# Inverse row sums of attention: turned by VectorE in 32x32 blocks and spread through DRAM, instead of turned by TensorE

## The chip, the cores and the metric

The program runs on one core of one Trainium2 chip. The metric is the device time of one execution in microseconds (us), median of several runs. Engines are named as in the profile: PE (TensorE, matmuls), PEld (its weight loads), DVE (VectorE), ACT (ScalarE), POOL (GpSimd), SP (SyncE, whose queue issues most transfers).

## The reference

Clustered attention, then two feed-forward layers. Batch 2, 8 heads, 768 tokens, head size 64, 16 clusters per head:

```
q_n, k_n, c_n = q, k, centroids, each row divided by (its norm + 1e-6)
mask    = argmax(q_n . c_n) == argmax(k_n . c_n)          # query and key in the same cluster
scores  = where(mask, q . k / 8, -1e9)
attn    = exp(scores - max(scores))
attn    = attn / (sum(attn) + 1e-9)                        # the row sums of this text
x       = (attn @ v) as [1536, 512]
x       = relu(x @ w_in)**2 @ w_out                        # first layer, 512 -> 2048 -> 512
out     = gelu_sigmoid(x @ w2_in) @ w2_out                 # second layer
```

## The kernel before

Sixteen (batch, head) problems are worked as 8 pairs of heads; a pair has two halves of 384 queries each, so there are 16 halves, n = 0 to 15. A half has three tiles of 128 queries for each of its two heads: six groups, 96 in all. Even n is the first half of a pair, odd n the second.

For each group PE multiplies queries by keys (`scores`, L615, and with the rest of the operands and the cluster masks as further rows L618), DVE takes the row maximum (`peak`, L624), ACT the exponential with the row sum beside it (`exponents`, L632), PE turns the 128x128 blocks of the exponentials (`turn`, L640), DVE and ACT copy them out of PSUM (`keep`, L648), and PE multiplies them by v (`values`, L658), into one PSUM bank for the half, with 64 partitions for each head and 384 columns for the queries.

The division by the row sum comes last. The sums of a half lie with queries on partitions: six columns, one for each group. The product lies with queries on columns. So the inverse sums must be turned and then copied to the 64 partitions of their head. Before, this is done in five steps: DVE adds 1e-9 and takes the reciprocal (`inverse`, L663 and L664); POOL copies each column 64 times side by side, 128x384 (`spread`, L669); PE turns that in three 128x128 transposes into a PSUM bank (`ratio`, L675); ACT copies the bank to a tile `rb` of 128x384 (`ratio_out`, L679); DVE multiplies the product by it on its way out of PSUM (`whole`, L696). `rb` has two buffers, and in some halves it also holds the result, which POOL's subtractions (`t_sum_first`, L715) read later.

Beside this runs the preparation of later pairs (`prep`): loads of q, k and v (L355), casts on ACT whose result is copied to other partitions by SP's transfers (`k_high` L443/L444, `q_high` L453/L454), subtractions on POOL (`k_low` L448, `q_low` L458), assignments to clusters (`aff` L476 and L479 on PE, `aff_out` L485 on ACT, `back` L493 on PE, `back_out` L503), a square root as a power on POOL (`root`, L507), the inverse norms (`inv_norm`, L513 and L514), `scale` (L526, POOL), `most` (L534), `less` (L537, POOL), `first`, `least`, `one_hot` (L541, L545, L552), `mask` (L559) and `mask_out` (L575 on ACT, then four copies by SP, L580).

The order on each engine is written by hand: every step has a key, in units of a group (about 2.3 us), and all steps are issued in the order of the keys; each engine takes its own in that order, and SP its transfers. Keys of a half are relative to `ORIGIN + 6 * n`, those of a pair to `12 * p`. Waits between engines are put in by the framework, by the memory that steps read and write. PSUM has two double-bank tiles for scores ("S") and four single banks ("T") for all else in this stage, the transposes of `ratio` among it.

After the attention both layers are matmuls from end to end, with the weights rebuilt from 64-bit words on ACT, DVE and POOL. The weights of the first layer begin to come in (L266) while the last pairs are still at work.

Of the kernel before, what the change touches and what calls it, by code (L numbers as in the profile page):

```python
# [8 lines left out]
F32 = mybir.dt.float32  # L9
# [7 lines left out]
P = 128  # L17
# [9 lines left out]
    scores=(0.0, 0.3), peak=(0.5, 0.7), exp=(0.85, 1.5), turn=(2.64, 2.85, 3.06), keep=(3.3, 3.2, (3.6, 3.8)),  # L27
)
HALVES = dict(
    values=(9.3, 9.6, 11.3, 11.6, 13.3, 13.6), inverse=(7.4, 6.02), spread=(7.45, 6.03), ratio=9.85, ratio_out=10.15,  # L30
    whole=13.95, whole_high=14.0, whole_low=15.0,
)
PAIR = dict(
# [1 line left out]
    aff=(-15.15, -15.1), aff_out=(-14.95, -14.8), back=(-13.15, -13.1), back_out=(-12.95, -12.8),  # L35
    k_high=(-13.4, -6.9), k_low=(-12.95, -6.3), q_high=(-12.6, -10.7), q_low=(-12.2, -8.9),
    root=-12.7, inv_norm=-9.95, scale=-9.9, most=-8.98, less=-8.95, first=-6.98,
    least=-6.95, one_hot=-6.0, mask=(-5.15, -5.1), mask_out=(-4.95, -4.8),
)

LAST = dict(
    values=(97.1, 97.2, 97.3, 97.4, 97.5, 97.6), inverse=(95.9, 95.9), spread=(96.2, 96.2), ratio=97.05, ratio_out=97.4,
    whole=97.95, whole_high=98.0, whole_low=98.62,
)
FIRST = dict(
# [5 lines left out]
    one_hot=-48.0, mask=(-47.9, -47.7), mask_out=(-47.859, -47.659, -47.559, -47.459), table=-48.107,  # L51
# [31 lines left out]
def cluster_attention_then_two_ffns(  # L83
# [17 lines left out]
    nc = tc.nc  # L101
    B, H, D, S = q_t.shape
    C = centroids.shape[0] // H
    DM = H * D
    NT = S // P
    HALF = S // 2
    TH = NT // 2
    NP = H // 2
    PAIRS = [(b, hp) for b in range(B) for hp in range(NP)]
    NH = B * H  # L110
# [196 lines left out]

    with tc.manual_schedule():
        with ExitStack() as actx, ExitStack() as rctx:
            psum = actx.enter_context(tc.tile_pool(name="psum", bufs=1, space=bass.MemoryType.PSUM))  # L310
            def ps_s(name):
                return psum.tile([P, 2, 512], F32, tag="S", name=name, bufs=2)
# [4 lines left out]
            one = places  # L317
            two = Twice(places)
# [42 lines left out]
            load(0, "k")  # L361
            half = one.tile([P, NT, 2, 2], F32, name="half")
            nc.vector.memset(half, 0.5)
            unit = one.tile([P, 1], F32, name="unit")
            nc.scalar.activation(out=unit, in_=half[:, 0, 0, 0:1], func=AF.Sqrt)

# [60 lines left out]
            def at(key, f, *args):  # L427
                events.append((key, len(events), lambda: f(*args)))
# [172 lines left out]
            s_t, m_t, p_t, sum_t, pt_t, tp_t = {}, {}, {}, {}, {}, {}  # L601
# [47 lines left out]
                    out=pt_t[n][:, 4 * b:4 * b + 4, i * P:(i + 1) * P],  # L649
                    in_=tp_t.pop((k, b)).rearrange("p (a f) -> p a f", a=4))  # L650

            pv_t, rb_t = {}, {}

            def values(n, t):
                if t == 0:
# [3 lines left out]
                                     rhs=pt_t[n, j][:, t, :], start=(t == 0), stop=(t == NT - 1), skip_group_check=True)  # L659

            def inverse(n):
                rc = rb_t[n] = two.tile([P, NT], F32, tag="rc", name="rc", bufs=2)
                nc.vector.tensor_scalar_add(rc, sum_t[n], 1e-9)  # L663
                nc.vector.reciprocal(rc, rc)  # L664

            def spread(n):
                rc = rb_t[n]
                wide = rb_t[n] = two.tile([P, NT, D], F32, tag="wide", name="wide", bufs=1)
                nc.gpsimd.tensor_copy(out=wide, in_=rc.unsqueeze(2).to_broadcast([P, NT, D]))  # L669
# [62 lines left out]
            for k in range(NG // 2):  # L732
                begin = ORIGIN + 2 * k
# [3 lines left out]
                for b in range(3):  # L737
                    at(begin + GROUP["turn"][b], turn, k, b)
                    when = GROUP["keep"][b]
                    at(begin + (when if b < 2 else when[k % 2 == 0]), keep, k, b)  # L740
            for n in range(NH):
                when, begin = (LAST, 0.0) if n == NH - 1 else (HALVES, ORIGIN + 6 * n)
                for t in range(NT):
                    at(begin + when["values"][t], values, n, t)
                for name, f in (("inverse", inverse), ("spread", spread), ("ratio", ratio), ("ratio_out", ratio_out),
                                ("whole", whole), ("whole_high", whole_high), ("whole_low", whole_low)):
                    if n % 2 == 0 or n % 8 > 3 or name[:6] != "whole_":
                        late_low = name == "whole_low" and n % 8 in (5, 7) and n < NH - 1
                        at(begin + (when[name][n % 2] if name in ("inverse", "spread") else when["whole"] + 0.7 if late_low else when[name]), f, n)
                if n % 2:  # L750
                    for i, name in enumerate(("T1",) if n % 8 < 4 else ("T2", "T3", "T4")):
                        at(begin + when["whole"] + (T_SUM_LAST[i] if n == NH - 1 else T_SUM + 0.1 * i), t_sum_first, n, name)
# [307 lines left out]
            for j in range(MJ):  # L1060
# [8 lines left out]
                else:  # L1069
                    t = u0 + 14 * BLOCK * (j - 1)  # L1070
# [8 lines left out]
            _, done = second_hidden(u1)  # L1079

            jobs = []
            for m in range(MF):
                jobs.append((y0 - 5 + 2 * m, 0, 1, m))
                j, i = divmod(m, 2)
# [7 lines left out]
            for j in range(MJ):  # L1092
                add, split12, split34 = sums_of(j)
                if j == 0:
                    begin = (y0 + 39, y0 + 46.1, y0 + 47.1)
                elif j == 1:
                    begin = (u1 + 2.3, u1 + 0.5 * (done["P5", 0] + 0.3), u1 + 0.5 * (done["P3", 0] + 0.3))
                else:
                    s = u1 + 0.5 * done["P4", j - 2]
                    begin = (s + 4.6, s + 5.2, s + 5.6)  # L1100
# [14 lines left out]
            for layer, begin in enumerate((y0, y1)):  # L1115
                u, n = begin, 0
# [72 lines left out]
```

## Time and profile before

| | us |
|---|---|
| median of 3 runs | 758.69 |
| lowest and highest | 757.93, 758.74 |
| profiled execution | 758.31 |
| its span | 756.5 |
| PE busy in the span | 746.7 (99%) |
| DVE busy | 526.5 (70%) |
| ACT busy | 461.2 (61%) |
| POOL busy | 166.3 (22%) |

Times of engines come from the profiled execution; the span runs from its first to its last instruction, and what lies around it makes the rest of its 758.31 us. A busy PE is not PE at its peak: matmuls are pipelined, so the time from one matmul's start to the next counts, not the duration of one. The clock granted to PE is full in all 40 slices of the span.

### The profile page before, as it was taken

How to read it: one execution, taken by the hardware profiler on the slowest of the kernel's cores; microseconds unless marked ns; L12 is line 12 of the kernel's file. 1: busy time of each engine (PE TensorE's matmuls, PEld its weight loads, DVE VectorE, ACT ScalarE, POOL GpSimd, SP SyncE). 2: the span in 40 equal slices, each digit the busy share in tenths (PEclk: the TensorE clock that was granted, in tenths of full speed). 3: DMA queues.
4: the chain of work that ended last, by engine and by line, in shares of the span. 5: the costliest groups of instructions: out<-in, count | busy, mean ns of one | idle time of the engine just before them, and what ended most of it. 6: DMA issues, size and time to landing. Idle time of an engine off the chain costs nothing.

```text
span 756.5 us, 10808 instructions
## 1 busy us (share of the span) xinstructions
PE 746.7 (99%) x4010; PEld 607.5 (80%) x4010; DVE 526.5 (70%) x939; ACT 461.2 (61%) x799; POOL 166.3 (22%) x139
## 2 busy tenths in 40 slices
PE   8899999999999999999999999999999999999998
PEld 6677776767767799999988888888888888888886
DVE  6886866867897667765787769754777677776321
ACT  7877777786787478776844435554656565443321
POOL 4765756775749130000000000000000000000000
PEclk9999999999999999999999999999999999999999
DMA  5132321322330122200232320100212212230201
GB/s 190 43 105 59 94 80 43 96 64 72 94 92 2 59 108 63 106 20 37 84 106 89 112 84 19 39 28 29 84 56 84 83 56 93 102 113 29 111 1 55
DMA packets 16900, 54.53 MB, mean 72 GB/s; under 512 B 2576, under 2 KB 2576, under 8 KB 15824
## 3 DMA queue, kind: packets, MB, share of 16 engines
q1 hardware_dynamic: 16560, 53.19, 22.1%
q8 instruction: 31, 0.51, 0.3%
q10 hardware_dynamic: 288, 0.66, 0.2%
q14 instruction: 21, 0.17, 0.1%
HBM read 43.02 MB, written 3.15 MB: 61 GB/s over the span
## 4 chain that ended last, share of the span: by engine, by line
PE 92%; DVE 4%; ACT 2%; POOL 1%; issue 0%; DVEq 0%; POOLq 0%; ACTq 0%
PE bank L996 35%; PE row L807 13%; PE bank L884 10%; PE ps_v L658 8%; PE ps_p L640 7%; PE bank L893 6%; PE ps_s L615 5%; PE ps_s L618 4%; DVE arena L624 2%; PE ps_aff L476 1%; PE ps_h L807 1%; ACT arena L632 1%; PE ps_r L675 1%; PE warm L392 1%; PE ps_back L493 1%; PE ps_oh L559 1%
## 5 line engine op out<-in xcount | busy, mean ns | idle before, releaser
L996 PE MATMUL bank<-arena 128*128 128x512 f32 x1152 | 261.6, 389 | 0.0
L996 PEld LDWEIGHTS bank<-arena 128*128 128x128 f32 x1152 | 216.2, 188 | 45.0 <-DVE arena L983 0.2
L624 DVE TENSOR_SCALAR_CACHE_REDUCE arena<-ps_s 128x768 bf16<-128x768 f32 x96 | 91.7, 955 | 38.6 <-PE ps_s L618 11.1
L979 ACT CAST arena<-arena 128x512 fp32r<-128x512 f32 x96 | 59.5, 620 | 86.0 <-PE bank L996 85.6
L807 PE MATMUL row<-arena 128*128 128x384 f32 x630 | 109.7, 334 | 0.4 <-ACT arena L825 0.4
L807 PEld LDWEIGHTS row<-arena 128*128 128x128 f32 x630 | 109.2, 188 | 0.7 <-ACT arena L825 0.7
L632 ACT ACTIVATE arena<-ps_s,arena 128x768 f32<-128x768 f32 x96 | 87.1, 908 | 35.1 <-DVE arena L624 34.8
L983 DVE TENSOR_TENSOR arena<-arena,arena 128x512 fp32r<-128x512 f32 x96 | 66.1, 689 | 60.3 <-ACT arena L979 60.0
L884 PE MATMUL bank<-arena 128*128 128x512 f32 x336 | 80.9, 389 | 0.0
L884 PEld LDWEIGHTS bank<-arena 128*128 128x128 f32 x336 | 63.1, 188 | 13.1
L658 PE MATMUL ps_v<-arena 128*64 128x384 f32 x384 | 72.3, 498 | 0.0
L640 PE MATMUL ps_p<-arena 128*128 128x128 f32 x576 | 70.8, 272 | 0.0
L244 ACT CAST arena<-arena 128x512 fp32r<-128x512 f32 x48 | 29.8, 620 | 64.4 <-DVE arena L240 64.4
L640 PEld LDWEIGHTS ps_p<-arena 128*128 128x128 f32 x576 | 65.7, 141 | 2.3 <-issue 0.6
L615 PE MATMUL ps_s<-arena 128*128 128x384 f32 x192 | 54.9, 367 | 2.4 <-ACT arena L632 2.2
L247 DVE TENSOR_TENSOR arena<-arena,arena 128x512 fp32r<-128x512 f32 x48 | 33.2, 692 | 24.0 <-ACT arena L244 23.2
L618 PE MATMUL ps_s<-arena 80*128 80x384 f32 x192 | 49.8, 340 | 0.1
L893 PE MATMUL bank<-arena 128*128 128x512 f32 x192 | 48.1, 389 | 0.0
L615 PEld LDWEIGHTS ps_s<-arena 128*128 128x128 f32 x192 | 31.0, 189 | 20.3 <-ACT arena L632 10.6
L648 DVE COPY arena<-ps_p 128x512 f32<-128x512 f32 x72 | 47.0, 678 | 0.2 <-PE ps_p L640 0.2
L658 PEld LDWEIGHTS ps_v<-arena 128*64 128x64 f32 x384 | 23.4, 136 | 25.5 <-issue 25.4
L648 ACT COPY arena<-ps_p 128x512 f32<-128x512 f32 x72 | 41.9, 582 | 0.5 <-PE ps_p L640 0.5
(135 smaller groups left out, 950.6 us busy)
## 6 DMA issues: line engine op xcount, KB each, us to landing
arena<-in_w_dram SPq DMA_DIRECT2D x48, 512.0 KB, 3.2
arena<-in_w_dram SPq DMA_DIRECT2D x8, 1024.0 KB, 4.9
arena<-arena SPq DMA_DIRECT2D x32, 192.0 KB, 2.5
arena<-in_k_t_dram SPq DMA_DIRECT2D x8, 384.0 KB, 4.0
arena<-in_v_dram SPq DMA_DIRECT2D x8, 384.0 KB, 3.2
out_dram<-arena SPq DMA_DIRECT2D x11, 256.0 KB, 2.1
arena<-in_q_t_dram SPq DMA_DIRECT2D x7, 384.0 KB, 3.4
arena<-arena SPq DMA_DIRECT2D x28, 48.0 KB, 2.1
```

Of the source, the lines that this page charges most:

```text
L615: nc.tensor.matmul(ps[:, n, :HALF], lhsT=x_s[i][:, t * P:(t + 1) * P], rhs=k1_s[i][:, n * HALF:(n + 1) * HALF], start=True, stop=False)
L618: nc.tensor.matmul(ps[:, n, :HALF], lhsT=q2_s[i][:, t * P:(t + 1) * P], rhs=k2_s[i][:, n * HALF:(n + 1) * HALF], start=False, stop=True)
L624: nc.vector.tensor_scalar(out=unused, in0=s_t[g][:, :, :HALF], scalar1=-scale, scalar2=None, op0=ALU.mult, op1=ALU.min, accum_out=m_t[g])
L632: nc.scalar.activation(out=p_t[g].rearrange("p (n f) -> p n f", n=2), in_=s_t.pop(g)[:, :, :HALF], func=AF.Exp, bias=m_t.pop(g), scale=sca ...
L640: nc.tensor.transpose(ps[:, x * P:(x + 1) * P], p_t[2 * k + j][:, t * P:(t + 1) * P], ident)
L648: (nc.scalar.copy if on_act else nc.vector.tensor_copy)(out=pt_t[n][:, 4 * b:4 * b + 4, i * P:(i + 1) * P], in_=tp_t.pop((k, b)).rearrange ...
L658: nc.tensor.matmul(pv_t[n][j * D:(j + 1) * D, :HALF], lhsT=raw[n // 2, "v"][:, j, t, :], rhs=pt_t[n, j][:, t, :], start=(t == 0), stop=(t ...
L807: nc.tensor.matmul(ps, lhsT=w[:, a, (off + x) * P:(off + x + 1) * P], rhs=FIRST_MOVING[moving, b][x][:, e, :], start=(n == 0 and name in ( ...
L884: nc.tensor.matmul(ps, lhsT=w[:, a, off + x * P:off + (x + 1) * P], rhs=MOVING[moving][x][:, b, :], start=(n == 0 and name in ("P1", "P2", ...
L893: nc.tensor.matmul(ps, lhsT=w[:, a, kk * P:(kk + 1) * P], rhs=THIRD_CHUNK[kk][:, b, :], start=(n == 0), stop=(n == 11), skip_group_check=True)
L983: nc.vector.tensor_tensor(out=t[:, 1, :], in0=g_t[m][:, c, :], in1=t[:, 0, :].bitcast(F32), op=ALU.subtract)
L996: nc.tensor.matmul(ps, lhsT=lhsT, rhs=rhs, start=(m == 0 and e == 0), stop=(m == MF - 1 and e == 2))
```

## The change

For all halves but the last, the steps between `inverse` and `whole` are others. `inverse` writes its six columns into a tile of 128x32 (in the order first head, second head), of which the other columns were set to zero once. A new step `send` has DVE transpose that tile in blocks of 32x32, so that each group of 32 partitions holds six rows of 32 inverse sums, and SP writes them in four transfers (6 rows x 128 bytes each) to a tile in DRAM of 6 rows x 128. `spread` then reads, for each head, its three rows as one of 384 and copies it to the head's 64 partitions of `rb`, in two transfers. `whole` is as before. `ratio` and `ratio_out`, PE's transposes and ACT's copy, and POOL's copy are left to the last half alone (`wide_rows`). Keys: `send` at 7.5 (even halves) and 6.1 (odd), `spread` at 9.9 and 9.0. In the preparation of pairs from the third on, `one_hot` moves from -6.0 to -6.4, which puts it ahead of one row maximum in DVE's order.

```diff
--- before.py
+++ after.py
@@ -27,7 +27,7 @@
     scores=(0.0, 0.3), peak=(0.5, 0.7), exp=(0.85, 1.5), turn=(2.64, 2.85, 3.06), keep=(3.3, 3.2, (3.6, 3.8)),
 )
 HALVES = dict(
-    values=(9.3, 9.6, 11.3, 11.6, 13.3, 13.6), inverse=(7.4, 6.02), spread=(7.45, 6.03), ratio=9.85, ratio_out=10.15,
+    values=(9.3, 9.6, 11.3, 11.6, 13.3, 13.6), inverse=(7.4, 6.02), send=(7.5, 6.1), spread=(9.9, 9.0),
     whole=13.95, whole_high=14.0, whole_low=15.0,
 )
 PAIR = dict(
@@ -35,11 +35,11 @@
     aff=(-15.15, -15.1), aff_out=(-14.95, -14.8), back=(-13.15, -13.1), back_out=(-12.95, -12.8),
     k_high=(-13.4, -6.9), k_low=(-12.95, -6.3), q_high=(-12.6, -10.7), q_low=(-12.2, -8.9),
     root=-12.7, inv_norm=-9.95, scale=-9.9, most=-8.98, less=-8.95, first=-6.98,
-    least=-6.95, one_hot=-6.0, mask=(-5.15, -5.1), mask_out=(-4.95, -4.8),
+    least=-6.95, one_hot=-6.4, mask=(-5.15, -5.1), mask_out=(-4.95, -4.8),
 )
 
 LAST = dict(
-    values=(97.1, 97.2, 97.3, 97.4, 97.5, 97.6), inverse=(95.9, 95.9), spread=(96.2, 96.2), ratio=97.05, ratio_out=97.4,
+    values=(97.1, 97.2, 97.3, 97.4, 97.5, 97.6), inverse=(95.9, 95.9), wide=96.2, ratio=97.05, ratio_out=97.4,
     whole=97.95, whole_high=98.0, whole_low=98.62,
 )
 FIRST = dict(
@@ -307,6 +307,7 @@
 
     with tc.manual_schedule():
         with ExitStack() as actx, ExitStack() as rctx:
+            dram = ctx.enter_context(tc.tile_pool(name="dram", bufs=2, space=bass.MemoryType.DRAM))
             psum = actx.enter_context(tc.tile_pool(name="psum", bufs=1, space=bass.MemoryType.PSUM))
             def ps_s(name):
                 return psum.tile([P, 2, 512], F32, tag="S", name=name, bufs=2)
@@ -361,6 +362,9 @@
             load(0, "k")
             half = one.tile([P, NT, 2, 2], F32, name="half")
             nc.vector.memset(half, 0.5)
+            inverse_p, turned_p = ([one.tile([P, 32], F32, name=f"{name}_{i}") for i in range(2)] for name in ("inverse", "turned"))
+            for t in inverse_p:
+                nc.gpsimd.memset(t, 0.0)
             unit = one.tile([P, 1], F32, name="unit")
             nc.scalar.activation(out=unit, in_=half[:, 0, 0, 0:1], func=AF.Sqrt)
 
@@ -649,7 +653,7 @@
                     out=pt_t[n][:, 4 * b:4 * b + 4, i * P:(i + 1) * P],
                     in_=tp_t.pop((k, b)).rearrange("p (a f) -> p a f", a=4))
 
-            pv_t, rb_t = {}, {}
+            pv_t, rb_t, sums_d = {}, {}, {}
 
             def values(n, t):
                 if t == 0:
@@ -659,11 +663,29 @@
                                      rhs=pt_t[n, j][:, t, :], start=(t == 0), stop=(t == NT - 1), skip_group_check=True)
 
             def inverse(n):
-                rc = rb_t[n] = two.tile([P, NT], F32, tag="rc", name="rc", bufs=2)
-                nc.vector.tensor_scalar_add(rc, sum_t[n], 1e-9)
+                if n == NH - 1:
+                    rc = rb_t[n] = two.tile([P, NT], F32, tag="rc", name="rc")
+                    nc.vector.tensor_scalar_add(rc, sum_t[n], 1e-9)
+                    nc.vector.reciprocal(rc, rc)
+                    return
+                rb_t[n], rc = inverse_p[n % 2], inverse_p[n % 2][:, :NT]
+                nc.vector.tensor_scalar_add(rc.rearrange("p (j t) -> p j t", j=2), sum_t[n].rearrange("p (t j) -> p j t", j=2), 1e-9)
                 nc.vector.reciprocal(rc, rc)
 
+            def send(n):
+                turned, to = turned_p[n % 2], dram.tile([NT, P], F32, tag="sums_d", name="sums_d")
+                nc.vector.transpose(out=turned, in_=rb_t.pop(n))
+                sums_d[n] = to
+                for x in range(4):
+                    nc.sync.dma_start(out=to[:, 32 * x:32 * x + 32], in_=turned[32 * x:32 * x + NT])
+
             def spread(n):
+                rb_t[n] = two.tile([P, HALF], F32, tag="rb", name="rb")
+                for j in range(2):
+                    nc.sync.dma_start(out=rb_t[n][j * D:(j + 1) * D],
+                                      in_=sums_d[n][TH * j:TH * j + TH].rearrange("t q -> (t q)").unsqueeze(0).to_broadcast([D, HALF]))
+
+            def wide_rows(n):
                 rc = rb_t[n]
                 wide = rb_t[n] = two.tile([P, NT, D], F32, tag="wide", name="wide", bufs=1)
                 nc.gpsimd.tensor_copy(out=wide, in_=rc.unsqueeze(2).to_broadcast([P, NT, D]))
@@ -742,11 +764,13 @@
                 when, begin = (LAST, 0.0) if n == NH - 1 else (HALVES, ORIGIN + 6 * n)
                 for t in range(NT):
                     at(begin + when["values"][t], values, n, t)
-                for name, f in (("inverse", inverse), ("spread", spread), ("ratio", ratio), ("ratio_out", ratio_out),
-                                ("whole", whole), ("whole_high", whole_high), ("whole_low", whole_low)):
+                for name, f in (("inverse", inverse), ("send", send), ("spread", spread), ("wide", wide_rows), ("ratio", ratio),
+                                ("ratio_out", ratio_out), ("whole", whole), ("whole_high", whole_high), ("whole_low", whole_low)):
+                    if name not in when:
+                        continue
                     if n % 2 == 0 or n % 8 > 3 or name[:6] != "whole_":
                         late_low = name == "whole_low" and n % 8 in (5, 7) and n < NH - 1
-                        at(begin + (when[name][n % 2] if name in ("inverse", "spread") else when["whole"] + 0.7 if late_low else when[name]), f, n)
+                        at(begin + (when[name][n % 2] if type(when[name]) is tuple else when["whole"] + 0.7 if late_low else when[name]), f, n)
                 if n % 2:
                     for i, name in enumerate(("T1",) if n % 8 < 4 else ("T2", "T3", "T4")):
                         at(begin + when["whole"] + (T_SUM_LAST[i] if n == NH - 1 else T_SUM + 0.1 * i), t_sum_first, n, name)
```

## Rows read from the trace of the kernel before

**Rows 1.** The page: engine, busy us, share of the span, instructions.

```profile
PE 746.7 (99%) x4010; PEld 607.5 (80%) x4010; DVE 526.5 (70%) x939; ACT 461.2 (61%) x799; POOL 166.3 (22%) x139
```

**Rows 2.** Busy time by stretches: window, length, PE, PEld, DVE, ACT, POOL, clock.

```profile
101.08:130.79 29.71, 29.69 (x205) 20.91 (x203) 22.37 (x46) 23.05 (x49) 20.77 (x15) 1.00 0.29 74
```

**Rows 3.** Line L675: ns of one (least/median/most), first and last start.

```profile
L675 PE MATMUL ps_r<-arena x48: 272/273/332, 35.4 to 250.8; 128*128 128x128 f32 x48
```

**Rows 4.** The chain of waits, 95 to 110 us: start, us held, what.

```profile
95.49 0.48 PE ps_r L675 x3
```

**Rows 5.** The chain of waits, 104 to 121 us.

```profile
105.96 0.54 PE ps_s L615 x2
...
110.32 0.48 PE ps_r L675 x3
110.80 0.35 PE ps_s L615 x2
```

**Rows 6.** Timeline of all engines, 107 to 126 us: start, us, engine, line.

```profile
108.87 1.64 DVE L708 TENSOR_TENSOR arena<-arena,arena 128x384 fp32r<-128x384 f32 x1
...
114.83 0.92 ACT L632 ACTIVATE arena<-ps_s,arena 128x768 f32<-128x768 f32 x1
...
115.89 0.30 PEld L615 LDWEIGHTS ps_s<-arena 128*128 128x128 f32 x2 [0.33 <-ACT arena L632]
...
119.05 0.91 ACT L632 ACTIVATE arena<-ps_s,arena 128x768 f32<-128x768 f32 x1
...
120.64 0.36 PEld L615 LDWEIGHTS ps_s<-arena 128*128 128x128 f32 x2
```

**Rows 7.** Timeline of POOL, 99 to 125 us.

```profile
101.79 0.51 POOL L669 COPY arena<-arena 128x384 f32<-128x384 f32 x1 [6.94 <-PE ps_back L493]
...
104.05 4.16 POOL L507 TENSOR_TENSOR arena<-arena 128x24 f32<-128x24 f32 x1
108.28 1.82 POOL L458 TENSOR_TENSOR arena<-arena,arena 64x768 fp32r<-64x768 f32 x1
...
124.53 1.00 POOL L715 TENSOR_TENSOR arena<-arena 128x384 f32<-128x384 f32 x1
```

**Rows 8.** DVE by form, 30 to 255 us: busy us, mean ns, idle before.

```profile
L708 DVE TENSOR_TENSOR arena<-arena,arena 128x384 fp32r<-128x384 f32 x7 | 11.6, 1651 | 0.0
...
L552 DVE TENSOR_TENSOR arena<-arena 128x384 fp32r<-128x384 f32 x7 | 3.9, 555 | 0.0
...
L664 DVE RECIPROCAL arena<-arena 128x6 f32<-128x6 f32 x16 | 3.1, 192 | 0.5
```

**Rows 9.** Timeline of DVE behind an odd and an even reciprocal.

```profile
102.54 0.96 DVE L624 TENSOR_SCALAR_CACHE_REDUCE arena<-ps_s 128x768 bf16<-128x768 f32 x1 [0.92 <-PE ps_s L618]
...
121.01 0.96 DVE L624 TENSOR_SCALAR_CACHE_REDUCE arena<-ps_s 128x768 bf16<-128x768 f32 x1 [0.48 <-PE ps_s L618]
```

**Rows 10.** Timeline of SP's queue: start, us of issuing, transfers.

```profile
37.52 2.46 SPq L580 DMA_DIRECT2D arena<-arena  x4
...
122.24 2.45 SPq L580 DMA_DIRECT2D arena<-arena  x4
```

**Rows 11.** Transfers by line: count, KB each, median us to landing.

```profile
arena<-arena SPq DMA_DIRECT2D x28, 48.0 KB, 2.1
...
arena<-in_w_dram SPq DMA_DIRECT2D x8, 1024.0 KB, 4.9
```

**Rows 12.** Timeline of DVE, PE and ACT at the places where transfers are awaited.

```profile
32.53 0.19 DVE L664 RECIPROCAL arena<-arena 128x6 f32<-128x6 f32 x1
...
42.74 0.52 PE L618 MATMUL ps_s<-arena 80*128 80x384 f32 x2
...
135.70 0.56 DVE L696 TENSOR_TENSOR arena<-ps_v,arena 128x384 f32<-128x384 f32 x1 [0.20 <-PE ps_v L658]
...
237.01 0.19 DVE L664 RECIPROCAL arena<-arena 128x6 f32<-128x6 f32 x1
...
248.10 1.17 ACT L270 ACTIVATE arena<-arena 128x1024 f32<-128x1024 f32 x1
```

## Prediction

> **What bounds the kernel now.** I read the busy table of the page first. There TensorE (PE) is occupied 99% of the span [rows 1]. But that is a mean over stages, and the change touches only the attention, which ends near 260 us. So next I read the busy time by stretches, over one period of the attention loop (one pair of heads, two halves, 29.71 us): PE 29.69, VectorE (DVE) 22.37, ScalarE (ACT) 23.05, GpSimd (POOL) 20.77 us [rows 2]. A busy PE is not yet PE at its peak, so third I read the chain of waits over two half-periods: it runs through PE steps, one behind the other [rows 4, 5]. The reader is to see there that every PE step has its slot, and that a step taken out closes up unless something else is late. What is late next shows in the timeline: in each period one score matmul waits 0.33 us (0.17 of it beyond the usual reload) for an exponential on ACT [rows 6].
>
> **What is removed, and what it is worth.** The three transposes of a half (L675) go in 15 of 16 halves, 45 of 48 [rows 3]. Their duration there, 273 ns, is latency; their slot on the chain is what counts.
> - In an even half they stand between two groups of assignment matmuls and hold the chain 0.48 us [rows 4]. The same groups run on directly where nothing is between them, so I take 0.48 for each of halves 2, 4, 6, 8, 10: 5 x 0.48 = 2.4 us.
> - In an odd half they stand ahead of the scores. They hold 0.48 us, but the two score matmuls behind them then take 0.35 where they take 0.54 without transposes ahead [rows 5]: the weight load that the transposes covered comes into the open. Net 0.48 - 0.19 = 0.29. Halves 1, 3, 5, 7, 9, 11 give 1.7 us, halves 12, 13, 14 (no assignment matmuls beside them) 0.9 us.
> - Half 0 lies in the start of the pipeline; I take the odd figure, 0.3 us.
> Sum of the slots: 2.4 + 1.7 + 0.9 + 0.3 = 5.3 us. The ACT copy (L679) and the POOL copy (L669, 0.51 us) [rows 7] go too; neither engine is on the chain, so by themselves they are worth nothing.
>
> **What takes some of it back.** The late exponential hangs on a chain that doesn't pass the transposes: DVE subtraction L708 (1.64 us), then L513, L514, POOL L526, DVE L534, the row maxima, two exponentials (the second from 114.83), and only then the score matmul at 115.89 [rows 6]. Were this chain as long as now, PE would come 0.29 us earlier to the odd half and wait 0.29 us longer. It gets shorter, though. L708 takes 1.64 us in the loop while L552, an operation of the same shape with two inputs in the same memory, takes 0.555 [rows 8]; L708 ends 0.4 us behind POOL's L458 (108.28 + 1.82 = 110.10, against 108.87 + 1.64 = 110.51) [rows 6, 7]. L458 starts when L507 is done (104.05 + 4.16 = 108.21), and L507 sits in a queue that begins with the POOL copy at 101.79 which the change removes [rows 7]. Without it that queue moves up by about 0.25 us (not the whole 0.51, since the next operation waits for an ACT cast, and L458's own cast is not earlier), L708 ends as much earlier, and the odd gain stays but for some 0.05 us: -0.3 us over six halves.
> The GPSIMD Engine Reference of the Trainium skill, section Key points, says that GpSimd shares its SBUF interfaces with DVE and that DVE instructions with two SBUF inputs contend. The trace agrees: 1.64 against 0.555 us. By the rule the odd gain is kept; without it rival B follows.
> Halves 12 and 13 lie where the weights of the first layer are prepared on DVE and ACT besides, and PE waits for them there. I count both slots as lost: -0.6 us.
>
> **What is added.** DVE: one 32x32-block transpose of a 128x32 tile per half. No row shows one. Nearest from below is the reciprocal of 128x6 with 0.192 us, from above L552 with 0.555, which moves twelve times as many columns [rows 8]; I take 0.2, being nearer in size to the first. DVE stands idle 0.92 us behind the odd reciprocal, 0.48 behind the even one [rows 9], so 0.2 is hidden in both; at 0.555 an even half would lose 0.08, half a microsecond in all. A gain from it is excluded, since it does nothing that was done before.
> SP: six transfers a half, four of 768 bytes to DRAM, two back with 64 copies of a row. None of this shape is in the trace. Issue: the four mask copies need 2.45 us, 0.6 each [rows 10]; four sends 2.4 us, two spreads 1.2. Landing: 2.1 us after issue for 48 KB, 4.9 for 1 MB [rows 11]; I take 2.1 both ways, since the small one is nearer, and 4.9 as the upper end.
> Behind the sends of an even half stand load_v and the mask copies. The sends begin at about 120.3 (the reciprocal plus 0.2) and end at 122.7, so the mask copies, now from 122.24 [rows 10], are issued by 125.5 and land by 127.6; the scores that need them come at about 131.5, 29.7 us behind the same place of the pair before: 4 us to spare. The spread waits for the sends (124.8) and for the POOL subtractions that still read its buffer (up to three of 1.0 us from 124.53 [rows 7], so to 127.5), is issued by 128.8 and lands by 131, and the product that reads it is at 135.70 [rows 12]: nearly 5 us to spare. Odd halves have more. So in the loop SP costs nothing. Two places are tighter.
> - Half 0: the sends begin near 33 (reciprocal at 32.53), end at 35.4, land at 37; the spreads then go from 37 to 38.3, ahead of the mask copies of pair 1, which now are issued from 37.52 [rows 10]. The last of them lands at about 42.3 instead of 41.5, and PE wants it at 42.74 less its gain [rows 12]. Bounds 0 to 1 us at 2.1 us landing; I take 0.3 lost.
> - Half 14: the load of the second weight block, which SP now issues as soon as it has nothing else to do, comes behind the sends of half 14 (reciprocal at 237.01): issued at 239.9, landed 4.9 us later, 244.8; ACT reads it at 248.10 [rows 12]. 3 us to spare; both ends move with the attention.
> The one-hot step (L552) passes one row maximum in the DVE order. That maximum comes at most L552's 0.555 us later [rows 8]; its exponential (119.05 to 119.96, and then its accumulator) is done some 0.6 us ahead of the weight load at 120.64 that waits for it [rows 6]. So I take nothing; were the cover gone, each tenth more would cost six tenths over the pairs.
>
> **Sum.** 5.3 - 0.3 - 0.6 - 0.3 = 4.1, and I add 0.2 for half 12 or 13 keeping part of its slot: 4.3 us. The stage after the attention waits for its results and moves as a whole. The profiled execution took 758.31 us (span 756.5), so 754.0; the median of the runs shown is 0.38 higher, and from it the forecast is 754.4.
>
> **Rivals.**
> - A, the forecast: PE slots close up, 754.4; own range 753.2 to 755.6.
> - B, the odd gain is lost: the chain through L708 doesn't shorten, so six odd halves give their 1.7 us to a longer wait for the exponential, and half 0 loses 1 us. Gain 5.3 - 1.7 - 0.6 - 1.0 = 2.0: 756.7. For it: the wait is there in each period. Against: POOL's queue reaches back to the removed copy.
> - C, slower: SP blocks ahead of other transfers while a write to DRAM lands. The place is pair 1's mask copies; from a landing time L of the sends (2.1 expected) on, PE waits L - 2.1 + 0.3 there, once. It overtakes the gain of 4.6 us (4.3 without the 0.3 taken for this place) from L = 6.4 on, above the 4.9 of the 1 MB load [rows 11], and at L = 8.5 the result is slower by 2.1 us: 760.8. Against: no row lands so late, and the loop itself bears even this. "DMA: Bandwidth & Descriptors" of the Trainium skill, section Rules for kernel authors, speaks against small transfers (under 64 KB mostly overhead); by it each of the 90 transfers pays its fixed cost, and by the rows this cost is hidden.
> - D, the change doesn't do what it says on the chain: gains within 1.5 us, because DVE and ACT set the pace as soon as PE is given 0.3 us; 757.7. Against: some 7 us of the period are free on each [rows 2].
>
> **Chances.** A 0.66, B 0.18, D 0.09, C 0.07. A difference below 0.2% (1.5 us) can't be told from none. Faster by more: A, and B but for its slow edge: 0.81. Same: D and that edge, 0.12. Slower: C, 0.07. The range goes from all slots kept and the reload between the assignment groups saved as well (5.3 + 0.4, and 0.4 of scatter: 752.6) to B's slow side, 757.3.
>
> **What would show it.** PE's slots without L675, period 29.71 us down to 28.9 to 29.0; L708 shorter than 1.64 and ending earlier behind the first maxima; the wait at the score matmul still near 0.33 (A) or near 0.6 (B); mask copies of pair 1 landing before their scores; DVE transposes near 0.2 us; the load of the second block near 235 and its reader not late. The prediction is wrong if the period stays, or if PE waits for a transfer in each of them.

## The result, and the profile after

| | before | after |
|---|---|---|
| median, us | 758.39 (4 runs) | 762.96 (4 runs) |
| lowest and highest | 757.93, 758.74 | 761.74, 763.83 |
| after : before | | 1.0059 [1.0042, 1.0077] |
| profiled execution | 758.31 | 763.83 |

The change makes the kernel slower by 4.6 us. The forecast was 4.3 us faster (754.4, range 752.6 to 757.3). The profiled execution of after took 5.2 us more of span. Its page (engine, busy us, share, instructions, then the granted clock in 40 slices):

```profile
span 761.7 us, 10852 instructions
PE 745.2 (98%) x3965; PEld 606.0 (80%) x3965; DVE 539.2 (71%) x954; ACT 455.4 (60%) x784; POOL 160.5 (21%) x126
PEclk9989999999999999999999999999999999999999
```

Against [rows 1] PE has its 45 transposes less, ACT and POOL are less busy, and DVE has 12.7 us more, although the change gave it 15 small transposes only. The third slice of PEclk is new: 8.

To see where the 5.2 us lie I cut the attention at the starts of one step that comes once a half, ACT's cast of the keys (L443 before, L447 after), and took the lengths between them, in us. The last two rows are a kernel without the fault that is found below, and the fastest one.

| kernel | half 0 | odd halves | even halves 2 to 10 | last interval |
|---|---|---|---|---|
| before | 10.63 | 14.77 to 14.80 | 14.93 to 14.95 | 15.34 |
| after | 13.60 | 14.52 to 14.54 | 15.21, 15.47, 15.87, 16.23, 15.18 | 15.10 |
| e4 | 10.53 | 14.53 to 14.54, one 14.79 | 14.32 to 14.36 | 15.08 |
| e5 | 10.32 | 14.51 to 14.54 | 14.31 to 14.35, one 14.66 | 15.09 |

After against before: half 0 +2.97, the even halves +3.25 together, five odd ones -1.27, the last interval -0.24; what follows it is +0.52 (551.46 against 550.94 us), what goes before it -0.03. Sum +5.20. So the odd halves do gain, as forecast, and the even ones, where the forecast's largest term lay, lose. The same stretches of after by engine (window, length, PE, PEld, DVE, ACT, POOL, clock): half 0, five microseconds of it, an odd half, an even half.

```profile
30.94:44.54 13.60, 11.46 (x60) 9.20 (x62) 8.67 (x17) 8.66 (x20) 3.62 (x2) 0.75 0.25 60
37.00:42.00 5.00, 4.82 (x21) 4.30 (x20) 1.73 (x4) 2.94 (x7) 0.00 (x0) 0.53 0.55 137
104.28:118.82 14.54, 14.49 (x96) 10.69 (x94) 12.23 (x26) 11.44 (x25) 11.30 (x6) 1.00 0.41 110
118.82:134.69 15.87, 14.76 (x103) 9.72 (x103) 12.33 (x23) 10.86 (x23) 8.80 (x7) 1.00 0.28 62
```

In the odd half PE stands 0.05 us, in the even one 1.11. Who makes it wait, 60 to 220 us of after (waiting, for whom: total us, times, longest):

```profile
PE ps_oh L563 <- DVE arena L652: 4.2, 6, 1.2
PE ps_p L644 <- ACT arena L579: 0.9, 2, 0.5
PE ps_s L619 <- ACT arena L636: 0.6, 1, 0.6
PE ps_p L644 <- DVE arena L718: 0.5, 2, 0.3
```

The same view of before has two waits only: one of 0.6 us for DVE's copy and one of 0.6 us of the scores for ACT. So the change brings 3.6 us for the copy, 0.9 for ACT's L579 (`mask_out`) and 0.5 for `whole` (L718), and no transfer is in that view. Most of it is DVE being late: its copy L652, and `whole`. The next view is DVE in an even half of after (start, us, line), and behind it POOL in the same microseconds.

```profile
150.87 1.49 DVE L556 TENSOR_TENSOR arena<-arena 128x384 fp32r<-128x384 f32 x1
...
153.16 0.68 DVE L652 COPY arena<-ps_p 128x512 f32<-128x512 f32 x1
153.76 1.38 DVE L672 TENSOR_SCALAR arena<-arena 128x6 f32<-128x6 f32 x1
155.17 0.19 DVE L673 RECIPROCAL arena<-arena 128x6 f32<-128x6 f32 x1
155.40 0.21 DVE L677 STREAM_TRANSPOSE arena<-arena 128x32 f32<-128x32 f32 x1
155.86 0.56 DVE L718 TENSOR_TENSOR arena<-ps_v,arena 128x384 f32<-128x384 f32 x1 [0.25 <-PE ps_s L622]
```

```profile
150.12 1.81 POOL L452 TENSOR_TENSOR arena<-arena,arena 64x768 fp32r<-64x768 f32 x1 [1.44 <-ACT arena L447]
152.02 3.09 POOL L473 TENSOR_TENSOR arena<-arena 128x768 f32<-128x768 f32 x2
```

The one-hot step (L556) takes 1.49 us, not 0.555 [rows 8]: begun at 150.87, it ends at 152.36, 0.43 behind the end of POOL's L452 at 151.93. The addition of 1e-9 to 128x6 sums (L672) takes 1.38 us: it ends at 155.14, when POOL's second square ends (155.11). In an odd half, where POOL is idle at that moment, the same addition takes 0.17. The copy L652, which reads PSUM, and the reciprocal are not lengthened. Over the stage (DVE by form, 30 to 260 us: busy us, mean ns):

```profile
L672 DVE TENSOR_SCALAR arena<-arena 128x6 f32<-128x6 f32 x15 | 10.7, 716 | 6.5 <-ACT arena L636 6.5
L556 DVE TENSOR_TENSOR arena<-arena 128x384 fp32r<-128x384 f32 x7 | 9.4, 1341 | 0.0
L730 DVE TENSOR_TENSOR arena<-arena,arena 128x384 fp32r<-128x384 f32 x7 | 9.0, 1285 | 0.0
```

L730 answers to L708 in [rows 8] and is shorter by 0.37 us, the way the prediction said; the one-hot step costs 5.5 us more than before, the addition 7.2 (3.5 us for 16 of them before).

In half 0 the addition meets POOL's L452 of the second pair. The next row maximum comes later by it, ACT's exponential stands 2.00 us for that maximum, and PE stands for ACT's copy behind the exponential (POOL, DVE, PE):

```profile
31.84 3.69 POOL L452 TENSOR_TENSOR arena<-arena,arena 64x768 fp32r<-64x768 f32 x2 [1.66 <-ACT arena L447]
```

```profile
32.30 1.39 DVE L672 TENSOR_SCALAR arena<-arena 128x6 f32<-128x6 f32 x1
```

```profile
36.62 0.55 PE L563 MATMUL ps_oh<-arena 128*64 128x128 f32 x6 [1.79 <-ACT arena L652]
```

PE is idle 1.79 us, and behind it the granted clock is 0.53 from 37 to 42 us, near its lower level of 1.2 GHz, where before it is 1.00. So in this execution half 0 loses 3 us, of which 1.8 are the wait; that the clock makes the rest fits the four runs of after: 761.74 and 762.33 at a mean clock of 1.000, 763.58 and 763.83 at 0.998 and 0.995.

### The profile page after: what moved, and what is told of

Same layout as the page of the kernel before. It is cut to its first block, busy times and chain, and to the rows that moved or that the text cites. A ratio compares the mean times of both kernels' runs of the same rounds, so it can differ in the third digit from the quotient of the medians.

```text
span 761.7 us, 10852 instructions
## 1 busy us (share of the span) xinstructions
PE 745.2 (98%) x3965; PEld 606.0 (80%) x3965; DVE 539.2 (71%) x954; ACT 455.4 (60%) x784; POOL 160.5 (21%) x126
## 4 chain that ended last, share of the span: by engine, by line
PE 84%; DVE 7%; issue 2%; ACT 2%; POOL 1%; ACTq 0%; DVEq 0%; POOLq 0%
PE bank L1020 34%; PE row L831 13%; PE bank L908 10%; PE ps_v L662 6%; PE ps_p L644 6%; PE bank L917 6%; PE ps_s L619 4%; DVE arena L628 3%; PE ps_s L622 3%; DVE arena L652 2%; PE ps_h L831 1%; PE ps_aff L480 1%; PE ps_back L497 1%; ACT arena L636 1%; POOL arena L296 0%
## 5 line engine op out<-in xcount | busy, mean ns | idle before, releaser
L644 PE MATMUL ps_p<-arena 128*128 128x128 f32 x576 | 73.5, 276 | 1.5 <-ACT arena L579 0.9
L619 PEld LDWEIGHTS ps_s<-arena 128*128 128x128 f32 x192 | 31.5, 191 | 26.0 <-issue 12.7
L652 DVE COPY arena<-ps_p 128x512 f32<-128x512 f32 x72 | 47.0, 678 | 0.3 <-PE ps_p L644 0.2
L652 ACT COPY arena<-ps_p 128x512 f32<-128x512 f32 x72 | 41.8, 581 | 1.4 <-PE ps_p L644 1.4
```

The source lines that it names most:

```text
L619: nc.tensor.matmul(ps[:, n, :HALF], lhsT=x_s[i][:, t * P:(t + 1) * P], rhs=k1_s[i][:, n * HALF:(n + 1) * HALF], start=True, stop=False)
L644: nc.tensor.transpose(ps[:, x * P:(x + 1) * P], p_t[2 * k + j][:, t * P:(t + 1) * P], ident)
L652: (nc.scalar.copy if on_act else nc.vector.tensor_copy)(out=pt_t[n][:, 4 * b:4 * b + 4, i * P:(i + 1) * P], in_=tp_t.pop((k, b)).rearrange ...
```

## The experiments

The theory (I, in the expectations): DVE and POOL exclude each other for some DVE instructions, and the change sets two of them against POOL's work, in two ways that have nothing to do with its transfers. The new key of the one-hot step puts it beside L452. And the removed POOL copy (L669) used to wait for the reciprocal, and so held POOL's queue until DVE's addition was done; without it the squares (L473) or L452 come forward onto the addition. Rival K: the key alone. Rival S (C of the prediction): the transfers through DRAM and SP. Rival H, later: the copy's good lies in the hold itself and not in the addition. "Hold" means below that a POOL copy of one column of the inverse (128x1), read by nobody, is put behind the reciprocal again.

**e1, the key back:** after, with

```diff
-    one_hot=-6.4
+    one_hot=-6.0
```

> The changed kernel with the one-hot step back at its old key (-6.0), all else as changed. Theory I (a DVE instruction that reads SBUF through the interface it shares with POOL stands until POOL's instruction ends; the removed POOL copy let POOL's squares come forward against DVE): the one-hot then falls beside the squares instead of beside the subtraction, so it still takes about 1.5 us, the 128x6 addition still over 1 us, and the time stays at 762 to 766. Theory K (the moved key of the one-hot alone made the loss): the mask's wait goes, about 1 us in six pairs, and the time is 755 to 758. Theory S (SP's transfers through DRAM make the loss): no change, 763.

Measured: 756.61 us, 0.998 [0.9971, 0.9988]. That is K's number, and the sum of theory I was wrong. But the addition still stands, and half 0 still takes 12.91 us. DVE and POOL of e1 in an even half:

```profile
119.03 0.55 DVE L556 TENSOR_TENSOR arena<-arena 128x384 fp32r<-128x384 f32 x1
...
120.10 0.83 DVE L672 TENSOR_SCALAR arena<-arena 128x6 f32<-128x6 f32 x1
```

```profile
119.05 1.85 POOL L473 TENSOR_TENSOR arena<-arena 128x768 f32<-128x768 f32 x1
```

Here the one-hot step began 0.02 us ahead of the square, and it was the square that took longer (1.85 us, where the least of its kind takes 1.46). The one that began first was not lengthened. The twelve runs of e1 go with the clock as those of after do: 755.82 to 756.33 at a mean clock of 0.999 or 1.000, 756.89 to 758.74 at 0.994 to 0.998. The median lies between the two groups.

**e2, the key alone:** the kernel before, with one_hot at -6.4.

> The kernel before with the one-hot at the new key (-6.4) and nothing else changed. Theory I: the one-hot falls beside POOL's subtraction (1.82 us) and takes about 1.5 us in place of 0.555, the next row maximum and the copy behind it come about 1 us later and the mask's transposes wait for that copy: 0.7 to 1 us in each of six pairs, 762 to 764.5. Theory S: no change, 758.4 within 1.

Measured: 762.23 us, 1.005 [1.0038, 1.0062]. Nothing of the transfers is in this kernel. DVE by form, and PE's longest wait, of e2:

```profile
L552 DVE TENSOR_TENSOR arena<-arena 128x384 fp32r<-128x384 f32 x7 | 9.4, 1342 | 0.0
...
L663 DVE TENSOR_SCALAR arena<-arena 128x6 f32<-128x6 f32 x16 | 3.5, 218 | 6.6 <-ACT arena L632 6.6
```

```profile
PE ps_oh L559 <- DVE arena L648: 4.3, 6, 1.2
```

The key costs 3.7 us by itself: the one-hot step stands, the addition does not, and half 0 is as before (10.66).

**e3, the hold:** after, with

```diff
+            held = one.tile([P, 1], F32, name="held")
+            def hold(n):
+                nc.gpsimd.tensor_copy(out=held, in_=rb_t[n][:, :1])
...
-    inverse=(7.4, 6.02), send=(7.5, 6.1),
+    inverse=(7.4, 6.02), hold=(7.45, 6.03), send=(7.5, 6.1),
```

> The changed kernel with a POOL copy of one column (128x1) of the inverse sums put where the POOL copy of 128x384 was, so that POOL waits for DVE's reciprocal there again; the one-hot stays at its new key. Theory I: the 128x6 addition takes 0.16 us again in halves 0, 2, 4, 6, 8 and 10, half 0 no longer loses 3 us, but the one-hot still takes 1.5 us: 757 to 760. Theory S: no change, 763.

Measured: 758.36 us, 0.9998 [0.9989, 1.0007]. A copy of one column, of no use to anything, takes 4.6 us off the time. The addition in e3, DVE by form:

```profile
L672 DVE TENSOR_SCALAR arena<-arena 128x6 f32<-128x6 f32 x15 | 3.8, 254 | 5.7 <-ACT arena L636 5.7
```

Its mean falls from 716 to 254 ns; the one-hot step stays at 1345.

**e4, both:** the edits of e1 and e3 together, so that all of the change's transfers stay in.

> The changed kernel with both: POOL held by the copy of one column, and the one-hot at its old key (-6.0). The transfers through DRAM stay, PE's transposes stay out. Theory I: both DVE instructions are short again, the even halves keep their slot of about 0.48 us and the odd ones 0.25, and the time is what the prediction forecast: 753.5 to 755.5. Theory S: 763, or at best 758, since the transfers are all there.

Measured: 754.61 us, 0.9948 [0.9936, 0.996]: the forecast of 754.4. S is refuted, since each send and spread is in it. POOL of e4 in an even half:

```profile
118.79 0.18 POOL L678 COPY arena<-arena 128x1 f32<-128x1 f32 x1 [1.64 <-DVE arena L673]
118.93 2.90 POOL L473 TENSOR_TENSOR arena<-arena 128x768 f32<-128x768 f32 x2
```

The copy makes POOL wait 1.64 us for the reciprocal (L673), and the squares begin behind the addition, not beside it. From the four kernels after, e1, e3 and e4: the key costs 6.35 us without the hold (762.96 - 756.61) and 3.75 with it (758.36 - 754.61); the missing hold costs 4.60 with the new key and 2.00 with the old. With only the runs of after and e1 at a clock of 0.999 or more (near 762.0 and 755.9) the key costs 6.1 without the hold, and the missing hold 3.7 and 1.3. Either way the two faults together cost more than the sum of each alone, by 2.6 us in the medians. In the profiles 1.9 of it lie in the five even halves (15.18 to 16.23 us in after, 15.03 to 15.05 in e3, 14.31 to 14.98 in e1) and 0.7 in half 0; why is not shown.

**e5, no addition, key back, no hold:** after, with one_hot at -6.0 and, for halves 0 to 14,

```diff
-                nc.vector.tensor_scalar_add(rc..., sum_t[n]..., 1e-9)
-                nc.vector.reciprocal(rc, rc)
+                nc.vector.reciprocal(rc..., sum_t[n]...)
```

This leaves 1e-9 out; a row sum holds exp(0) of its maximum, so it is at least 1, and 1e-9 is below the last place of a 32-bit float there.

> The changed kernel with the one-hot at its old key and without the addition of 1e-9 in halves 0 to 14 (the reciprocal reads the row sums themselves, which are at least 1); no POOL copy holds anything. Theory I, narrowed by the first four runs (the 128x6 addition stands for POOL, the reciprocal of 0.19 us and the transpose of 0.21 us go on beside it): half 0 and the even halves lose nothing although POOL's work comes forward, 753.5 to 755. Rival H (any DVE instruction on SBUF at this place stands, and only holding POOL helps): the reciprocal takes the addition's wait and the time is 756 to 757, as with the one-hot back alone.

Measured: **752.58 us, 0.9924 [0.9912, 0.9936]**, the fastest of all, below what was expected and 5.9 us under the kernel before. H is refuted: nothing holds POOL's queue here. DVE and POOL of e5 in an even half:

```profile
116.98 0.18 DVE L672 RECIPROCAL arena<-arena 128x6 f32<-128x6 f32 x1
117.19 0.21 DVE L676 STREAM_TRANSPOSE arena<-arena 128x32 f32<-128x32 f32 x1
```

```profile
115.94 3.27 POOL L473 TENSOR_TENSOR arena<-arena 128x768 f32<-128x768 f32 x2
```

Reciprocal and transpose run from 116.98 to 117.40 in the middle of POOL's squares (115.94 to 119.21) and take no longer than with POOL idle. So it is the addition that must not meet POOL, not whatever reads the sums. The medians of e4 and e5 are 2.0 us apart, the two profiles 1.76. Of these half 0 explains 0.21, one odd half 0.27, and the stretch behind the last interval, where half 13's addition took 1.01 us in e4, 0.79; half 8 takes 0.34 more in e5, for no reason that was found. The largest rest, 0.73, lies ahead of half 0. That start differs among the ten kernels whatever their edits: half 0 begins between 30.59 us (e5) and 31.54 (e3), and in e7, which has the addition and the hold, at 30.63. So about 1 us is the addition's, not 2.

**e6, no addition, key as in after:**

> The changed kernel without that addition in halves 0 to 14, the one-hot at its new key. Theory I: the one-hot still stands for POOL's subtraction (about 1.5 us), so the even halves stay some 0.7 us longer than with it at the old key, as with POOL held (758.4): 757.5 to 759. Rival H: no gain over the change, 762 to 763.

Measured: 757.09 us, 0.9982 [0.9974, 0.9991], a little under what was expected. The one-hot step still takes 1340 ns, and PE's waits for L652 behind it are 4.3 us, as in e2. Against e5 the key costs 4.5 us.

**e7, the slots back:** e4, and three 128x128 transposes of the identity on PE per half (n = 0 to 14), read by nobody, at the place of `ratio`:

```diff
+            def fill(n):
+                ps = ps_t("ps_r")
+                for i in range(TH):
+                    nc.tensor.transpose(ps[:, i * P:(i + 1) * P], ident, ident)
...
+    fill=9.85,
```

> The kernel with POOL held and the one-hot back (754.6), and three 128x128 transposes of the identity on PE in each of halves 0 to 14 where the removed ones were; nobody reads them. This asks what PE's slots alone are worth. If the forecast's sum of the slots holds (0.48 to 0.6 in five even halves, 0.25 to 0.29 in the odd ones and the last, 4 to 5 us in all): 758 to 759.5. If something else made the gain of that kernel, such as the ACT copy or the POOL copy that went: 754.6 within 1.

Measured: 757.56 us, 0.9989 [0.998, 0.9998], 2.95 above e4 and less than the 4 to 5 us of the forecast's sum. The even halves take 14.92 to 14.95 us, 0.59 more each, 2.97 in five. The odd halves take what they take without the slots, and the stretch behind the last interval takes 0.38 more. The two profiles are only 2.62 apart, because e7 reaches half 0 0.70 us earlier (30.63 against 31.32), in the start that differs whatever the edits; that the medians differ by just the even halves' sum is chance. Why shows in PE's steps in an odd half, e4 first, then e7:

```profile
109.09 0.62 PE L619 MATMUL ps_s<-arena 128*128 128x384 f32 x2
...
113.46 0.62 PE L619 MATMUL ps_s<-arena 128*128 128x384 f32 x2
...
114.45 0.61 PE L619 MATMUL ps_s<-arena 128*128 128x384 f32 x2
...
115.26 0.93 PE L644 MATMUL ps_p<-arena 128*128 128x128 f32 x7
```

```profile
109.53 0.55 PE L690 MATMUL ps_r<-arena 128*128 128x128 f32 x3
109.83 0.60 PE L619 MATMUL ps_s<-arena 128*128 128x384 f32 x2
...
114.17 0.62 PE L619 MATMUL ps_s<-arena 128*128 128x384 f32 x2
...
114.98 0.55 PE L619 MATMUL ps_s<-arena 128*128 128x384 f32 x2
...
115.72 0.49 PE L644 MATMUL ps_p<-arena 128*128 128x128 f32 x3
```

From the place of the transposes to the score matmul of the next group it is 4.37 us without them and 4.64 with them: a slot of 0.27. From there to the turn it is 1.80 without and 1.55 with them: PE gives 0.25 back: ahead of 114.45 the weight load of e4 stands 0.34 us for ACT's exponential, as in [rows 6]. The odd slot is worth nothing.

**e8, before without the addition** (halves 0 to 14), the same edit as in e5 on the old code.

> The kernel before without the addition of 1e-9 in halves 0 to 14. It asks how much of the 2 us between the kernel without the addition (752.6) and the one with POOL held (754.6) belongs to the addition alone. Theory I: in the kernel before the addition stands for POOL only in half 13 (1.01 us; elsewhere 0.16), so 0.5 to 1 us: 757.5 to 758. If the addition's own time on DVE were on the path in each half, 15 x 0.2 us: 755.5.

Measured: 756.38 us against 758.12 in the same set, 0.9976 [0.9966, 0.9986]; more than expected. Its odd halves take 14.54 to 14.59 us with all PE slots in place, 0.22 less than before: the POOL copy begins as much earlier in the half, POOL's queue with it, and so the subtraction L708 (L711 here) and the exponential that the odd half waits for. POOL and DVE of e8 in the odd half that begins at 100.06:

```profile
100.56 0.50 POOL L672 COPY arena<-arena 128x384 f32<-128x384 f32 x1 [6.95 <-PE ps_back L493]
...
107.05 1.83 POOL L458 TENSOR_TENSOR arena<-arena,arena 64x768 fp32r<-64x768 f32 x1
```

```profile
107.84 1.45 DVE L711 TENSOR_TENSOR arena<-arena,arena 128x384 fp32r<-128x384 f32 x1
```

The copy begins 0.50 us and the subtraction L458 6.99 us behind the half's beginning; in before, in the half from 101.08, it is 0.71 and 7.20 [rows 7]. In after, with no copy, L458's counterpart begins 6.95 us behind it, and 6.95 too in e7 with its slots in place: that is where the odd gain of after comes from too. The one odd half of e4 and e7 without the gain (half 3, 14.79 and 14.78) fits: there the copy of one column begins 1.02 us behind the half's beginning in e4, where it begins 0.68 behind it in half 5.

## Why the prediction was wrong

**Right.** What bounds the kernel, and what the transposes are worth in even halves: 0.48 taken, 0.59 measured (e7). The transpose on DVE: 0.2 taken, 0.21 measured. The transfers are hidden: SP of after, four sends and two spreads of one half (start, us of issuing),

```profile
155.63 1.51 SPq L680 DMA_DIRECT2D sums_d<-arena  x4
...
161.24 1.11 SPq L685 DMA_DIRECT2D arena<-sums_d  x2
```

take 1.51 and 1.11 us where 2.4 and 1.2 were counted, and PE waits for none of them. The number itself, once the two faults are undone, is e4's 754.61, and the period of a pair is 28.9 us, as the prediction said. In part that is luck. Set part by part against before, the profile of e4 gains 3.0 us in the even halves (2.4 forecast; 0.4 more for a reload was in the range), 1.2 in the odd ones and the last interval (1.4 forecast, for another reason), 0.1 in half 0 (0 forecast) and nothing behind them (0.5 forecast), and loses 0.35 ahead of half 0.

**Right by the wrong sum.** The odd halves: 0.29 from PE's slot, kept because POOL's queue moves up by 0.25. The slot is worth 0 (e7), as in the mechanism of rival B, and the queue alone gives the 0.22 to 0.25 (e8).

**Wrong, the step that decided.** Two sentences cost an edit at nothing. Of the one-hot step: "So I take nothing", with the maximum behind it "at most L552's 0.555 us later". In e2 it takes 1.39 to 1.49 us in the six pairs whose key moved, because the move puts it beside POOL's subtraction (1.34 is the mean with the second pair, whose key stays, at 0.557). The path was wrong as well: the prediction measured its cover at the scores' weight load, but PE waits at the mask's transposes (`ps_oh`) for DVE's copy behind the delayed maximum, 4.3 us in six waits in e2 against one of 0.6 in before. The even halves of e2 are 0.70 us longer each, and the key costs 3.7 us in all. And of the removed copies: "neither engine is on the chain, so by themselves they are worth nothing". The POOL copy is not on the chain, but its wait for the reciprocal was an order: POOL's later work could not start before DVE had its sums. That is worth 2.0 us (e1 against e4), and 4.6 with the new key (after against e3); both are less without the clock's part, see e4. The only way to a slower kernel that the prediction weighed was C, the transfers; none of its rivals set DVE against POOL by the change itself.

What should have led there stood in [rows 8]: 1.64 against 0.555 us for two instructions of one shape. The prediction read that difference rightly as DVE against POOL, and then used it for the one instruction that the change frees, not for the two that it brings into POOL's way. Those two stand in the trace of before, DVE and POOL of an even half, which the prediction had not laid side by side:

```profile
118.64 0.56 DVE L552 TENSOR_TENSOR arena<-arena 128x384 fp32r<-128x384 f32 x1
...
119.71 0.16 DVE L663 TENSOR_SCALAR arena<-arena 128x6 f32<-128x6 f32 x1
```

```profile
116.77 1.82 POOL L448 TENSOR_TENSOR arena<-arena,arena 64x768 fp32r<-64x768 f32 x1 [1.44 <-ACT arena L443]
120.26 0.50 POOL L669 COPY arena<-arena 128x384 f32<-128x384 f32 x1 [1.67 <-PE ps_oh L559]
120.72 2.89 POOL L469 TENSOR_TENSOR arena<-arena 128x768 f32<-128x768 f32 x2
```

The one-hot step begins 0.05 us behind the end of L448 (118.59). Whatever puts it ahead of a maximum of 0.96 us puts it into L448. The addition lies in the 1.67 us in which POOL stands ahead of its copy; the profile names a PE step for that wait, but the copy begins 0.16 us behind the reciprocal's end, and e4's copy names the reciprocal. Without the copy L469 begins in those 1.67 us. Even the price of the second fault was there: in half 13 of before the addition begins at 220.25, while POOL's L291 runs from 219.40 to 221.23, and takes 1.01 us; in the other fifteen halves it takes 0.16 to 0.17.

"SBUF — State Buffer" of the Trainium skill, section SBUF: two separate sides, says of a DVE instruction with two SBUF inputs, or in a mode that uses both ports, and a GpSimd instruction, that whichever starts first gets the shared ports for the whole instruction and the other is blocked. The runs agree on both sides: the one-hot step ends 0.43 us behind L452 in after, and the square takes 1.85 us behind the one-hot step in e1.
"VectorE: DVE Perf Modes" of the Trainium skill, section Mode 2×_2P — use both read ports for one tensor, says that this mode, on both read ports, is how a tensor_scalar on 32-bit data gets its double rate. That fits the addition with its one input, which stands; no run here turned the mode off, so that it is the reason is not shown.

**Half 0** was taken at no change, 0.3 us gained by its slot and 0.3 lost to the SP queue; it is 3.0 us longer. The transfers have no part in it: e4 has them and takes 10.53 us. It is the addition beside L452, and then the clock: e3 and e4 keep the two apart, e5 and e6 have no addition, and their half 0 takes 10.3 to 10.5 us.

## What to carry to other kernels

A step that is removed may have been worth nothing for what it did and something for what it waited for: ask which work of its engine comes forward without it, and beside whom. For every step that is moved, by key or by queue, look up what the other engine does in that microsecond (POOL for a step of DVE, DVE for one of POOL), small instructions included; different durations for one shape in the trace are the sign. And a slot on the busiest engine is worth its length only in those stretches where nothing else is nearly late: 0.59 us in even halves, 0 in odd ones.

## What the runs showed of the hardware

- A DVE addition on 128x6 elements, 0.17 us by itself, takes up to 1.39 us beside a POOL subtraction or square (after); a reciprocal of the same size (0.18) and a 32x32-block transpose of 128x32 (0.21) are not lengthened (e5).
- The one that begins later is lengthened: the one-hot step took 0.55 us and POOL's square 1.85 when the step began 0.02 us ahead of it (e1); it took 1.49 us when it began 0.75 us behind POOL's subtraction (after).
- PE's idle 1.79 us in half 0 was followed by a granted clock of 0.53 over 37 to 42 us and 0.79 over 42 to 47 (0.68 and 0.97 in e1); in e3 to e6, whose half 0 takes 10.3 to 10.5 us, it was 1.00 there.
